# Pooling the keys on TensorE, and another start, in an attention and MLP kernel

## The chip, the cores and the metric

The kernel runs on one core of one Trainium2 chip. The metric is the device time of one execution in microseconds (us). The core has five engines that run their own instruction streams in order and wait for each other by semaphores: TensorE (PE, matrix multiply; PEld is its loading of weights), VectorE (DVE), ScalarE (ACT), GpSimd (POOL) and SyncE (SP). POOL and SP also issue the memory transfers (DMA) of this kernel; the rows POOLq and SPq are these issues. 128 is the number of partitions of the two on-chip memories, SBUF and PSUM; TensorE writes PSUM only.

## The reference

```python
def _attn_ref(q, kv, w_sr):              # q (4, 12288, 128), kv (4, 384, 32, 128)
    r = 4
    kv_pool = kv.reshape(B, H // r, r, W // r, r, C).mean(axis=(2, 4))
    kv_flat = kv_pool.reshape(B, -1, C) @ w_sr         # 768 keys of 128 per batch
    k = v = kv_flat
    s = (q @ k.transpose(0, 2, 1)) / np.sqrt(C)
    a = np.exp(s - s.max(-1, keepdims=True))
    a /= a.sum(-1, keepdims=True) + 1e-09
    return a @ v

def _moe_ref(x, w_in, w_out):            # x (49152, 128), d_ff 2048
    h = x @ w_in
    g = h * (1.0 / (1.0 + np.exp(-1.702 * h)))
    return g @ w_out
```

Each of four batches has 12288 queries and an image of 384 x 32 positions; 4 x 4 positions are averaged to one key, so a batch has 96 x 8 = 768 keys, which serve as values too. All 49152 attention outputs go through one MLP with 2048 hidden channels.

## The kernel before

Queries are worked on in 96 groups of 512. Four groups are a supergroup (2048 queries, 24 of them), and 24 groups are a batch. The 768 keys of a batch are six columns of 128, taken three at a time, so a group is two units (t = 0 and 1) and attention has 192 units. The MLP has 512 units of the same size.

A unit is filled and later drained. `fill_attn` (L171) lets TensorE write three 128 x 512 blocks of scores into a PSUM tile of the pool `big` (two tiles), and ACT takes the exponential of all three into an SBUF tile `ag` (14 tiles). `drain_attn` (L183) multiplies these with the values, six matmuls adding up in a PSUM tile of the pool `ring` (two tiles), and DVE multiplies the sum with the reciprocal row sums and writes it to `xs` (L193). `sums` (L196) is called once per supergroup: 24 matmuls with a narrow matrix of ones (32 columns, one of four column tiles of TensorE for each group) give the row sums in a ring tile, DVE transposes and inverts them (L206 to L210), and POOL spreads them over the partitions (L213) into `rb` (three tiles).

The main loop (L293) fixes the order by hand: step n fills unit n + 2 and drains unit n - 10; after every eighth step come the sums. `manual_schedule` keeps each engine's instructions in the order in which the code is written. `background` (L216), called before each even unit, adds what prepares the next data:

- Queries: `cast_q` (L75) copies a supergroup of q from f32 to bf16 in DRAM, issued on POOL two supergroups ahead. `load_qT` (L80) reads it back transposed into `qT` (two tiles), issued on SP one supergroup ahead.
- Keys of the next batch: `load_kv` (L64) loads an eighth of the image (96 partitions x 2048 f32) on SP into one of three tiles `kvt`. `pool_kv` (L101) adds the 4 x 4 positions with four DVE instructions (L106 to L109). When all eight are done, `transpose_pooled`, `make_k` and `make_v` (L114, L122, L134) transpose on TensorE, multiply with `w_sr` and copy the results to `kT` and `v`; keys and values pass through tiles of `big`.

The start is different for batch 0. POOL issues the cast of the first 512 queries and the first three key loads (cast to bf16 on the way), and then makes the identity matrix `ident`. TensorE pools and transposes at once by multiplying each of the 16 positions of a tile with `ident` and adding up in PSUM (L146 to L157). All 768 keys are made before the first scores. Then come the casts of the other queries of the first supergroup and of the next, and the two weight matrices of the MLP (L160 to L166).

The MLP (`fill_moe`, `drain_moe`, `store`, L243 to L276) starts when the last attention unit is filled, and the change does not touch it.

## Time and profile before

| | us |
|---|---|
| median of three runs | 1095.76 (1087.45 to 1108.19) |
| profiled execution | 1080.91 |
| its span, first to last instruction | 1079.1 |
| queue of hardware transfers (SP), share of 16 engines' span | 23.3% |
| queue of software transfers (POOL), the same | 9.7% |
| mean granted TensorE clock | 0.983 |

Times from the trace, and all sums with them, refer to the profiled execution, whose span is 16.7 us below the median of the three runs. A page of the profile gives busy times by engine, the span in slices, the chain of work that ended last, and groups of instructions by source line with their count, busy time, mean duration in ns and the idle time of the engine before them with its releaser. The other views used below are the timeline (start, duration, instruction, and in brackets the idle time before it and what ended it), the waits (total, how often, longest), and windows (busy time of each engine in a stretch, granted clock, DMA share, GB/s written).

### The profile page before, as it was taken

What the parts mean: (1) busy time and instruction counts of PE and PEld (TensorE: products, weight loads), DVE (VectorE), ACT (ScalarE), POOL (GpSimd) and SP (SyncE); (2) the same over time, 40 slices, a digit from 0 to 9 for tenths busy, and PEclk for the clock granted to TensorE, in tenths of its full rate; (3) what the DMA queues carried; (4) which work ended last, traced back from release to release, by engine and by line L of the source; (5) the groups of instructions that cost most, each with busy time, mean ns of one, the idle gap of its engine ahead of it and who ended that gap; (6) DMA issues with size and microseconds to landing.
All of it is one profiled execution on the core that took longest, in us unless ns stands there. A gap on an engine that the chain in (4) does not pass through costs nothing.

```text
span 1079.1 us, 13408 instructions
## 1 busy us (share of the span) xinstructions
PE 1004.4 (93%) x5368; PEld 461.7 (43%) x5368; DVE 319.0 (30%) x471; ACT 955.2 (89%) x707; POOL 111.6 (10%) x137
## 2 busy tenths in 40 slices
PE   2379978988999999999999999999999999999998
PEld 2224433433444444444444444444444444444443
DVE  0058477347633322222211221122112211221112
ACT  0178877767889999999999999999999999999997
POOL 2124234214323210000000000000000000000000
PEclk9889999989999999999999999999999999999999
DMA  7999399499544001110011101110111101110111
GB/s 109 152 198 186 68 198 184 59 202 167 100 72 85 20 10 40 39 39 36 34 39 39 40 30 39 40 40 31 38 40 39 37 33 39 39 40 30 39 40 39
DMA packets 79790, 74.33 MB, mean 69 GB/s; under 512 B 54496, under 2 KB 57696, under 8 KB 79328
## 3 DMA queue, kind: packets, MB, share of 16 engines
q1 hardware_dynamic: 73520, 56.70, 23.3%
q0 software_dynamic: 6208, 16.78, 9.7%
q8 instruction: 42, 0.69, 0.3%
q14 instruction: 20, 0.16, 0.1%
HBM read 52.49 MB, written 37.75 MB: 84 GB/s over the span
## 4 chain that ended last, share of the span: by engine, by line
PE 83%; DMA 11%; ACT 3%; issue 2%; DVE 1%; SPq 0%; POOL 0%; ACTq 0%; POOLq 0%; DVEq 0%
PE big L247 30%; PE ring L261 30%; PE big L177 9%; PE ring L189 9%; DMA qT<-q_bf 7%; DMA kvt<-in_kv_dram 3%; PE ring L201 2%; ACT ag L180 2%; PE ring L273 2%; ACT ag L250 1%; DMA q_bf<-in_q_dram 1%; DVE kvt L106 0%; SPq L83 0%; ACTq L334 0%; POOL kvt L67 0%
## 5 line engine op out<-in xcount | busy, mean ns | idle before, releaser
L250 ACT ACTIVATE ag<-big 128x1536 bf16<-128x1536 f32 x512 | 689.3, 1555 | 4.7 <-PE big L247 4.6
L247 PE MATMUL big<-x,w_in_sb 128*128 128x512 bf16 x1536 | 414.7, 379 | 0.0
L261 PE MATMUL ring<-ag,w_out_sb 128*128 128x512 bf16 x1536 | 414.2, 379 | 0.5 <-ACT ag L250 0.5
L180 ACT ACTIVATE ag<-big 128x1536 bf16<-128x1536 f32 x192 | 262.9, 1467 | 78.4 <-PE big L177 77.9
L261 PEld LDWEIGHTS <-w_out_sb 128*128 128x128 bf16 x1536 | 150.0, 98 | 181.9 <-issue 0.7
L247 PEld LDWEIGHTS <-w_in_sb 128*128 128x128 bf16 x1536 | 145.8, 98 | 162.4 <-issue 5.0
L265 DVE CAST oT<-ring 128x512 bf16<-128x512 f32 x96 | 66.4, 692 | 450.0 <-PE ring L261 450.0
L177 PE MATMUL big<-qT,kT 128*128 128x512 bf16 x576 | 161.9, 392 | 38.2 <-DMA qT<-q_bf 28.1
L189 PE MATMUL ring<-ag,v 128*128 128x512 bf16 x576 | 159.4, 388 | 7.8 <-DVE x L193 7.6
L213 POOL PARTITION_BROADCAST rb<-t x96 | 93.5, 1025 | 254.1 <-DVE t L210 201.1
L177 PEld LDWEIGHTS <-kT 128*128 128x128 bf16 x576 | 55.1, 100 | 117.6 <-issue 31.9
L193 DVE TENSOR_TENSOR x<-ring,rb 128x512 bf16<-128x512 f32 x96 | 65.2, 688 | 112.4 <-PE ring L189 111.1
L275 DVE CAST o_sb<-ring 128x512 f32<-128x512 bf16 x96 | 66.4, 692 | 101.6 <-PE ring L273 101.6
L189 PEld LDWEIGHTS <-v 128*128 128x128 bf16 x576 | 57.3, 99 | 79.9 <-issue 15.5
L273 PEld LDWEIGHTS <-oT 128*128 128x128 bf16 x384 | 32.2, 114 | 22.7 <-DVE oT L265 1.9
L106 DVE TENSOR_TENSOR kvt<-kvt 96x1024 f32<-96x1024 f32 x24 | 30.5, 1271 | 37.6 <-DMA kvt<-in_kv_dram 37.6
L273 PE MATMUL ring<-ident,oT 128*128 128x128 bf16 x384 | 37.2, 219 | 0.9 <-DVE oT L265 0.8
L201 PE MATMUL ring<-ag,ones 128*32 128x512 bf16 x576 | 35.5, 381 | 0.0
L152 PE MATMUL big<-ident,kvt 96*128 96x96 bf16 x128 | 11.3, 280 | 23.0 <-POOL ident masks.py:199 15.2
L130 ACT CAST kT<-big 128x384 bf16<-128x384 f32 x1 | 0.5, 479 | 34.0 <-DVE kT L129 34.0
L107 DVE TENSOR_TENSOR kvt<-kvt 96x512 f32<-96x512 f32 x24 | 23.4, 976 | 0.8
L201 PEld LDWEIGHTS <-ones 128*32 128x32 bf16 x576 | 13.2, 96 | 21.1 <-issue 10.6
(31 smaller groups left out, 115.7 us busy)
## 6 DMA issues: line engine op xcount, KB each, us to landing
out_dram<-o_sb SPq DMA_DIRECT2D x96, 256.0 KB, 2.0
kvt<-in_kv_dram SPq DMA_DIRECT2D x24, 768.0 KB, 8.6
q_bf<-in_q_dram POOLq DMA_DIRECT2D x23, 512.0 KB, 6.7
kvt<-in_kv_dram POOLq DMA_DIRECT2D x8, 384.0 KB, 6.4
w_in_sb<-in_moe_w_in_dram POOLq DMA_DIRECT2D x1, 512.0 KB, 11.4
w_out_sb<-in_moe_w_out_dram POOLq DMA_DIRECT2D x1, 512.0 KB, 25.4
qT<-q_bf SPq DMA_TRANSPOSE x25, 8.7
q_bf<-in_q_dram POOLq DMA_DIRECT2D x1, 384.0 KB, 7.2
```

The costliest lines, as they stand in the source:

```text
L177: nc.tensor.matmul(s_ps[:, k, :], kTs[b][:, jc * 128:(jc + 1) * 128], rhs, start=True, stop=True)
L180: nc.scalar.activation(a, s_ps, AF.Exp, scale=scale)
L189: nc.tensor.matmul(av_of[i], vs[b][:, jc, :], a_of[i, t][:, k, :], start=(jc == 0), stop=(jc == JC - 1))
L193: nc.vector.tensor_tensor(xs[s][:, (i % 4) * G:(i % 4 + 1) * G], av_of.pop(i), rb_of.pop(i), MUL)
L201: nc.tensor.matmul(ss[32 * gi:32 * gi + 32, :], ones, a_of[4 * s + gi, jc // K][:, jc % K, :], start=(jc == 0), stop=(jc == JC - 1))
L213: nc.gpsimd.partition_broadcast(rb, t2[32 * gi:32 * gi + 1, :])
L247: nc.tensor.matmul(h_ps[:, k, :], w_in_sb[:, fc * 128:(fc + 1) * 128], xs[g // 4][:, (g % 4) * G:(g % 4 + 1) * G], start=True, stop=True)
L250: nc.scalar.activation(a, h_ps, AF.Gelu_apprx_sigmoid)
L261: nc.tensor.matmul(o_of[g], w_out_sb[:, fc, :], a[:, k, :], start=(fc == 0), stop=(fc == FCH - 1))
L265: nc.vector.tensor_copy(oT.rearrange("p a b -> p (a b)"), o_of[g])
L273: nc.tensor.transpose(o_ps[:, gi * 128:(gi + 1) * 128], oT[:, :, gi], ident)
L275: nc.vector.tensor_copy(o_sb.rearrange("p a b -> p (a b)"), o_ps)
```

## The change

The edit has these parts:

1. Pooling moves from DVE to TensorE. A tile of keys is now 128 partitions (rows of the image) x 16 columns of it x 128 channels, in bf16. A matrix `mean4` (128 x 32, 1/16 where partition p belongs to pooled row p // 4) is the weight; four matmuls of 512 columns, one for each of four neighbouring image columns, add up to 32 pooled rows. Three tiles (`ch`) fill three column tiles of TensorE, 96 pooled rows, half of a batch's keys (`a`).
2. Keys and values are made by halves, with ring tiles of PSUM instead of big ones. For batches 1 to 3 the steps stand at fixed groups of the batch before (9, 10, 12, 13 for the first half, 17, 18, 20, 21 for the second), after the drain.
3. All key loads are issued on POOL, with a cast to bf16: six of 1 MB (f32) per batch, at groups 2, 4, 6, 11, 13, 15. For batch 0 they go to `xs` tiles that are written much later.
4. Batch 0 starts with the first half of its keys. The order of the first eight units is changed: t = 0 of groups 0 to 3, then t = 1 of them, and the second half of the keys is made before the fifth unit.
5. The queries of the first two supergroups (4096) are loaded straight to SBUF with a cast and transposed on TensorE; ACT copies the first four groups from PSUM, DVE the next four. For the others `load_qT` is issued two supergroups ahead (three `qT` tiles) and `cast_q` three ahead.
6. `ident` and `mean4` are made on POOL before any load. The MLP weights are loaded at groups 40 and 64. `ag` has 15 tiles.

```diff
-    kv_r = kv.rearrange("b (hp r1) (wp w1) c -> b wp hp r1 (w1 c)", r1=r, w1=r)
+    kv_r = kv.rearrange("b (ch p) (a w) c -> b a ch p (w c)", p=128, a=2)
...
-    qpool = ctx.enter_context(tc.tile_pool(name="qpool", bufs=2))
-    agpool = ctx.enter_context(tc.tile_pool(name="ag", bufs=14))
+    qpool = ctx.enter_context(tc.tile_pool(name="qpool", bufs=3))
+    agpool = ctx.enter_context(tc.tile_pool(name="ag", bufs=15))
...
+    def load_kv(b, a, ch):
+
+        t = xs[NS - 1 - a * HC - ch] if b == 0 else kvload.tile([128, SG], BF, name="kvt")
+        nc.gpsimd.dma_start(out=t, in_=kv_r[b, a, ch])
+        kv_tiles[b, a, ch] = t.rearrange("p (wp w1 c) -> p w1 wp c", w1=r, c=C)
+
+    def pool_kv(b, a):
+
+        ps = ring.tile([128, 512], F32, name="ring")
+        ts = [kv_tiles.pop((b, a, ch)) for ch in range(HC)]
+        order = ([(ch, w) for ch in range(HC) for w in range(r)] if b == 0 else
+                 [(ch, w) for w in range(r) for ch in range(HC)])
+        for ch, w in order:
+            nc.tensor.matmul(ps[32 * ch:32 * ch + 32, :], mean4, ts[ch][:, w],
+                             start=(w == 0), stop=(w == r - 1))
+        pooled[b, a] = kvtmp.tile([Hp, 4, C], BF, name="pooled")
+        nc.vector.tensor_copy(pooled[b, a].rearrange("p a c -> p (a c)"), ps[:Hp, :])
...
+    def transpose_q(g):
+        s = g // 4
+        if g % 4 == 0:
             qTs[s] = qpool.tile([128, 1, SG], BF, name="qT")
...
+        ps = ring.tile([128, 4, 128], BF, name="ring")
+        for i in range(4):
+            o = (g % 4) * G + i * 128
+            nc.tensor.transpose(ps[:, i, :], xs[NS // 2 + s][:, o:o + 128], ident)
+        dst = qTs[s][:, 0, (g % 4) * G:(g % 4 + 1) * G].rearrange("p (t i) -> p i t", i=4)
+        if s == 0:
+            nc.scalar.copy(dst, ps)
+        else:
+            nc.vector.tensor_copy(dst, ps)
...
+    load_q(0, 0, 1)
+    for ch in range(HC):
+        load_kv(0, 0, ch)
+    load_q(0, 1, 4)
+    for ch in range(HC):
+        load_kv(0, 1, ch)
+    load_q(1, 0, 4)
+    cast_q(2)
+    cast_q(3)
...
+    transpose_q(0)
+    pool_kv(0, 0)
+    transpose_pooled(0, 0)
+    make_k(0, 0)
+    load_qT(2)
...
-            if s + 1 < NS:
-                load_qT(s + 1)
-            if s + 2 < NS:
-                cast_q(s + 2)
...
+            if 3 <= s + 2 < NS:
+                load_qT(s + 2)
+            if 4 <= s + 3 < NS:
+                cast_q(s + 3)
+        if b + 1 < B and gb in (2, 4, 6, 11, 13, 15):
+            a, ch = divmod((2, 4, 6, 11, 13, 15).index(gb), HC)
+            load_kv(b + 1, a, ch)
...
+    units = [(i, t) for t in range(2) for i in range(4)] + [(i, t) for i in range(4, NG) for t in range(2)]
+
     def fill(n):
         if n < NA:
+            i, t = units[n]
             if n % 2 == 0:
                 background(n // 2)
-            fill_attn(n // 2, n % 2)
+            if n < 8:
+                if t == 0 and i > 0:
+                    transpose_q(i)
+                if n == 4:
+                    make_v(0, 0)
+                    pool_kv(0, 1)
+                    transpose_pooled(0, 1)
+                    make_k(0, 1)
+                if n == 6:
+                    make_v(0, 1)
+                if n == 7:
+                    transpose_q(4)
+                    transpose_q(5)
+            fill_attn(i, t)
...
+        elif n < NA and n % 2 == 1:
+            if n in (9, 11):
+                transpose_q(6 + (n - 9) // 2)
+            extra(n // 2)
```

The order of the instructions on three queues shows what moved. The rows give the line, the operation, what it writes and reads, its shape and the semaphores that it waits for (DMASW and DMAHW are those of transfers issued by software on POOL and by hardware on SP). On POOL, at the program's start, before:

```order
L77 DMA q_bf<-in_q_dram 16x4096
L67 DMA kvt<-in_kv_dram 96x4x512 x3
masks.py:197 MEMSET ident 128x128
masks.py:199 ISA
masks.py:199 AFFINE_SELECT ident<-ident 128x128 [waits Pool_49]
```

and on POOL at the same place now (mean_118 is `mean4`; x_99 and x_105 to x_110 are tiles of `xs` that hold queries and keys for a while):

```order
masks.py:197 MEMSET ident 128x128
masks.py:199 ISA
masks.py:199 AFFINE_SELECT ident<-ident 128x128 [waits Pool_49]
L145 MEMSET mean_118 128x32
L146 AFFINE_SELECT mean_118<-mean_118 128x32 [waits Pool_49]
L148 AFFINE_SELECT mean_118<-mean_118 128x32 [waits Pool_49]
L122 DMA x_99<-in_q_dram 128x512
L69 DMA x_110<-in_kv_dram 128x2048
L69 DMA x_109<-in_kv_dram 128x2048
L69 DMA x_108<-in_kv_dram 128x2048
```

The identity matrix stood behind the first four loads; now it and `mean4` stand ahead of every load. On SP, the first transposed queries and key loads before:

```order
L83 DMA_TRANSPOSE qT<-q_bf 128x1x2048 [waits DMASW2_49]
L70 DMA kvt<-in_kv_dram 96x4x512 [waits DMASW6_49,DMASW3_49,PE_49]
L70 DMA kvt<-in_kv_dram 96x4x512 [waits DMASW7_49,DMASW4_49,PE_49]
L70 DMA kvt<-in_kv_dram 96x4x512 [waits DMASW5_49,DMASW0_49,PE_49]
L70 DMA kvt<-in_kv_dram 96x4x512 [waits DMAHW4_49,DVE_49]
L83 DMA_TRANSPOSE qT<-q_bf 128x1x2048 [waits DMAHW1_49,DMAHW0_49,DMAHW2_49,DMASW5_49,PE_49]
```

and on SP now:

```order
L141 DMA w_sr_f<-in_w_sr_dram 128x128
L118 DMA_TRANSPOSE qT<-q_bf 128x1x2048 [waits DMASW1_49]
L118 DMA_TRANSPOSE qT<-q_bf 128x1x2048 [waits DMASW2_49,PE_49,Activation_49]
L118 DMA_TRANSPOSE qT<-q_bf 128x1x2048 [waits DMASW4_49,DVE_49,PE_49]
L118 DMA_TRANSPOSE qT<-q_bf 128x1x2048 [waits DMAHW1_49,DMASW7_49,PE_49]
```

The key loads that waited for DVE are gone from between the transposes. On DVE, between two supergroups while the keys of batch 1 are made, before:

```order
L106 TENSOR_TENSOR kvt<-kvt 96x1024 [waits DMASW5_49,DMAHW6_49,DMASW2_49,DMASW0_49]
L107 TENSOR_TENSOR kvt<-kvt 96x512 [waits DVE_49]
L108 TENSOR_TENSOR kvt<-kvt 96x256 [waits DVE_49]
L109 TENSOR_TENSOR pooled<-kvt 96x128 [waits DVE_49]
L193 TENSOR_TENSOR x_87<-ring,rb 128x512 [waits PE_49,Pool_49]
```

and on DVE now:

```order
L197 TENSOR_TENSOR x_88<-ring,rb 128x512 [waits PE_49,Pool_49]
L82 CAST pooled<-ring 96x512 [waits PE_49]
L197 TENSOR_TENSOR x_88<-ring,rb 128x512 [waits PE_49,Pool_49]
L90 COPY pT<-ring 128x384 [waits PE_49]
L197 TENSOR_TENSOR x_88<-ring,rb 128x512 [waits PE_49,Pool_49]
```

The additions that wait for a transfer ahead of a normalising multiply are gone; single copies that wait for TensorE take their place, and the wait for the key transfers is on TensorE's pooling matmuls (L79).

More of the change, by code (lines that the diff above doesn't have):

```diff
@@ new lines, in transpose_pooled, with make_k @@
+    def transpose_pooled(b, a):
+        ps = ring.tile([128, 4, Hp], BF, name="ring")
+        t = pooled.pop((b, a))
+        for wp in range(4):
+            nc.tensor.transpose(ps[:, wp, :], t[:, wp, :], ident[:Hp, :Hp])
+        pTs[b, a] = kvtmp.tile([128, h], BF, name="pT")
+        nc.vector.tensor_copy(pTs[b, a], ps.rearrange("p a b -> p (a b)"))
+    def make_k(b, a):
+        ps = ring.tile([128, 512], F32, name="ring")
+        if a == 0:
+            kTs[b] = kvres.tile([128, J], BF, name="kT")
+        nc.tensor.matmul(ps[:, :h], w_sr_sb, pTs[b, a], start=True, stop=True)
+        nc.vector.tensor_copy(kTs[b][:, a * h:(a + 1) * h], ps[:, :h])
@@ L73, with make_v, cast_q @@
+    def make_v(b, a):
+        ps = ring.tile([128, 512], F32, name="ring")
+        if a == 0:
+            vs[b] = kvres.tile([128, JC, C], BF, name="v")
+        pT = pTs.pop((b, a))
+        for k in range(K):
+            nc.tensor.matmul(ps[:, k * C:(k + 1) * C], pT[:, k * 128:(k + 1) * 128], w_sr_sb,
+                             start=True, stop=True)
+        nc.vector.tensor_copy(vs[b][:, a * K:(a + 1) * K, :].rearrange("p k c -> p (k c)"), ps[:, :h])
     qTs = {}
-    def cast_q(s, lo=0, n=SG):
-        sl = slice(s * SG + lo, s * SG + lo + n)
+    def cast_q(s):
+        sl = slice(s * SG, (s + 1) * SG)
@@ L134, in make_v @@
-    def make_v(b):
-        pT = pTs.pop(b)
-        v_ps = big.tile([128, K, 512], F32, name="big")
-        vs[b] = kvres.tile([128, JC, C], BF, name="v")
-        for jc in range(JC):
-            nc.tensor.matmul(v_ps[:, jc // 3, (jc % 3) * C:(jc % 3 + 1) * C],
-                             pT[:, jc * 128:(jc + 1) * 128], w_sr_sb, start=True, stop=True)
-        nc.vector.tensor_copy(vs[b].rearrange("p (a b) c -> p a (b c)", a=2), v_ps[:, 0:2, :h])
-    p_ps = big.tile([128, K, 512], F32, name="big")
```

111 lines of the change are left out of this document (30 added, 81 removed).

## The prediction

> **What bounds the kernel now.** I read the page first: busy shares, the granted clock by slice, the chain that ended last.
>
> ```profile
> span 1079.1 us, 13408 instructions
> PE 1004.4 (93%) x5368; PEld 461.7 (43%) x5368; DVE 319.0 (30%) x471; ACT 955.2 (89%) x707; POOL 111.6 (10%) x137
> ...
> PEclk9889999989999999999999999999999999999999
> ...
> PE 83%; DMA 11%; ACT 3%; issue 2%; DVE 1%; SPq 0%; POOL 0%; ACTq 0%; POOLq 0%; DVEq 0%
> ```
>
> TensorE is busy 93% of the span, and 11% of the chain is DMA. Where that 11% lies is read from the windows view (columns: stretch, its length, busy us of each engine with counts, granted clock, DMA share, GB/s).
>
> ```profile
> 186.60:193.20 6.60, 4.69 (x12) 1.64 (x12) 0.00 (x0) 2.03 (x2) 0.00 (x0) 0.50 0.65 119
> 64.33:379.22 314.89, 286.92 (x1699) 121.97 (x1699) 177.41 (x264) 252.55 (x186) 98.01 (x112) 0.97 0.72 128
> 379.22:1079.10 699.88, 694.48 (x3505) 325.47 (x3504) 138.68 (x201) 689.15 (x512) 2.91 (x4) 1.00 0.10 37
> ```
>
> The last 699.88 us (the MLP) have ACT busy for 689.15 and TensorE for 694.48: nothing to gain there, and the edit leaves them alone. 64.33 and 379.22 are where the first and the last of the 24 row-sum blocks start; the timeline gives the first, the chain of waits (start, duration, what) two late neighbours.
>
> ```profile
> 64.33 1.48 PE L201 MATMUL ring<-ag,ones 128*32 128x512 bf16 x24
> ```
>
> ```profile
> 355.43 1.41 PE ring L201 x24
> ...
> 367.36 1.41 PE ring L201 x24
> ```
>
> Undisturbed, one block follows another after 367.36 - 355.43 = 11.93 us. The 23 intervals should take 23 x 11.93 = 274.4, and they take 314.9: **40.5 us too many**. TensorE's waits in that stretch (view of waits: us in total, times, longest):
>
> ```profile
> PE big L177 <- DMA qT<-q_bf: 14.0, 4, 4.5
> PE ring L189 <- DVE x L193: 7.6, 2, 4.1
> PE big L177 <- ACT ag L180: 6.1, 7, 1.0
> PE ring L189 <- DVE t L206: 0.2, 1, 0.2
> ```
>
> That is 27.9. The other 12.6 are the key and value matmuls and matmuls at half clock after a wait: the 186.60 window shows a granted 0.50, so about half of its 4.69 busy us is lost. Without sums a group of eight units is 48 matmuls in 11.93 - 1.41 = 10.52, 0.219 each; keys and values are 2304 columns a batch, 4.5 such matmuls, about 1.0, and with their weight loads I say 1.1, or 3.4 for three batches. What lies ahead, 0 to 64.33, is the third pot: start-up.
>
> **What goes: the two kinds of waits.** The transposed queries are late because SP issues them one supergroup ahead, behind key loads that wait for buffers. Now SP issues nothing else during attention, two supergroups ahead, with a third buffer; casts run three ahead. The wait on the normalising multiply comes from DVE standing behind a key tile:
>
> ```profile
> 228.59 1.22 DVE L106 TENSOR_TENSOR kvt<-kvt 96x1024 f32<-96x1024 f32 x1 [4.84 <-DMA kvt<-in_kv_dram]
> ...
> 231.22 1.28 DVE L193 TENSOR_TENSOR x<-ring,rb 128x512 bf16<-128x512 f32 x2
> ...
> 231.96 1.44 PE L189 MATMUL ring<-ag,v 128*128 128x512 bf16 x3 [4.07 <-DVE x L193]
> ```
>
> DVE held L193 back for a late key tile and TensorE then waited 4.07. The four DVE additions per key tile are gone. Of the 6.1 on ACT, about 3.6 are the bubbles of key and value results in the pool that ACT drains; they move to the other PSUM pool. I keep 2.5, the filling of the pipeline.
>
> **What is added to TensorE.** Pooling now costs, for batches 1 to 3, six blocks of 12 matmuls, three abreast: four rounds. The 24 row-sum matmuls run four abreast, six rounds in 1.41, so a block is 4/6 x 1.41 = 0.94, and six are 5.6. If they ran singly a block would be 12 x 0.219 = 2.6; hidden it cannot be, as TensorE is the bound here; the row with the same tiling is nearest, so 0.94. Four query transposes per group go by the MLP's:
>
> ```profile
> L273 PE MATMUL ring<-ident,oT 128*128 128x128 bf16 x384 | 37.2, 219 | 0.9 <-DVE oT L265 0.8
> L201 PE MATMUL ring<-ag,ones 128*32 128x512 bf16 x576 | 35.5, 381 | 0.0
> L201 PEld LDWEIGHTS <-ones 128*32 128x32 bf16 x576 | 13.2, 96 | 21.1 <-issue 10.6
> ```
>
> 37.2 / 96 = 0.39 per group; two groups fall in this stretch, 0.8. Narrow weight loads take 96 ns and lie beside matmuls. The Trainium skill (TensorEngine Tiling (Array Packing), Key Properties and Restrictions) says that a change of tiling mode drains the array and that column tiling turns fast weight load off; if that laid the 12 loads of 96 ns of a block open, 1.15 x 6 = 6.9 us would come on top, 1064. The trace speaks against it: 24 loads of the same narrow form fit inside 1.41.
>
> **POOL's queue.** It gets 18 key loads of about 0.67 us issue time; DVE and TensorE wait for its partition broadcasts, which now stand behind loads that wait for a key buffer. A buffer is freed by pooling matmuls that stand two groups of queries ahead of the load, about 3 us (2 x 11.93 / 8), so I price this at nothing; that margin is its cover, and if it goes, broadcasts and then the multiply are late next. The stretch becomes 274.4 + 3.4 (keys, values) + 2.5 + 5.6 + 0.8 + 2.0 for waits that I can't name = **288.7**, against 314.9: 26.2 less. The 2.0 lies between 0 and a late tile at each of six blocks (rival 4).
>
> **Start-up.** It decides the rest, and here POOL's order matters. Timeline, POOL:
>
> ```profile
> 1.22 0.63 POOL L77 DMA_DIRECT2D q_bf<-in_q_dram  x1 [0.79 <-POOLq L323]
> 1.85 2.04 POOL L67 DMA_DIRECT2D kvt<-in_kv_dram  x3
> 3.88 0.22 POOL masks.py:197 MEMSET ident<- 128x128 bf16 x1
> ...
> 14.82 0.28 POOL masks.py:199 TENSOR_SCALAR_AFFINE_SELECT ident<-ident 128x128 bf16<-128x128 bf16 x1 [10.71 <-issue]
> ```
>
> The mask operation stands still for 10.71 us with nothing shown that it waits for. Before, four loads were already issued; now all loads stand behind it. The Trainium skill (GPSIMD Engine Reference, Instruction dispatch) has the first call of a freshly loaded kernel pay a code load of about 6 us that shows no instruction; by it the sum would be 4.7 lower.
>
> Loads then start at 1.22 + 0.22 + 10.71 + 0.28 + about 0.8 (three small mask operations, each at most 0.28) = 13.2. Rates by the windows view, and times from issue to landing (last column of the page's list of transfers):
>
> ```profile
> 20.00:25.00 5.00, 1.46 (x16) 1.25 (x16) 0.56 (x1) 0.00 (x0) 0.79 (x2) 1.00 1.19 191
> 304.00:306.00 2.00, 2.00 (x11) 0.89 (x10) 0.69 (x1) 2.00 (x3) 0.40 (x2) 1.00 1.49 262
> ```
>
> ```profile
> qT<-q_bf SPq DMA_TRANSPOSE x25, 8.7
> ...
> q_bf<-in_q_dram POOLq DMA_DIRECT2D x1, 128.0 KB, 3.1
> ```
>
> The first queries (128 KB) land 3.1 later, at 16.3. Three key tiles of 0.52 MB at 191 GB/s take 8.2: 24.5 (at 262 GB/s, 22.3). I take 191, the rate of key loads. The chain from there goes by these rows:
>
> ```profile
> 34.10 0.52 PE L127 MATMUL big<-pT,w_sr_sb 128*128 128x384 bf16 x1
> 34.34 0.56 DVE L157 CAST pT<-big 128x384 bf16<-128x384 f32 x1 [10.49 <-PE big L152]
> ...
> 36.06 0.48 ACT L130 CAST kT<-big 128x384 bf16<-128x384 f32 x1 [34.05 <-DVE kT L129]
> ...
> 37.12 2.72 PE L177 MATMUL big<-qT,kT 128*128 128x512 bf16 x6 [1.05 <-DVE v L141]
> ...
> 38.59 2.79 ACT L180 ACTIVATE ag<-big 128x1536 bf16<-128x1536 f32 x2 [2.06 <-PE big L177]
> 53.88 2.74 PE L177 MATMUL big<-qT,kT 128*128 128x512 bf16 x6 [14.04 <-DMA qT<-q_bf]
> ```
>
> TensorE is slow here (0.45 us a matmul against 0.22 later). The last tile's four pooling matmuls 1.8, cast 0.7 (0.56 x 512/384), transposes 0.4, copy 0.56, key matmul 0.5, cast 0.56, first scores 1.36: 30.4. Three more units, each exp 1.40, query copy on ACT 0.6 (0.48 x 512/384) and scores 1.36 in a row, since one engine does both copy and exp: 40.5 cold, 38.4 with scores at 0.66; 39.5. Then the second half of keys, landed by 24.5 + 1.96 MB / 191 GB/s = 34.8: values, 12 pooling matmuls (2.6 to 5.4), casts, keys, scores, together 8.2: 47.7. Four exps of 1.345 (689.15 / 512) and the tenth unit's scores: **first sums at 53.7**, say 53, against 64.33, where 14.04 were a wait for queries.
>
> **Sum.** 53.0 + 288.7 + 699.9 = 1041.6, against 1079.1: 37.5 less. The profiled execution itself took 1080.91 and the three runs shown 1087 to 1108, median 1095.76; I carry the difference over, 1095.76 - 37.5 = 1058, and say 1057.
>
> **Rivals.**
> 1. *The pause at the mask is shorter*, because four loads ran beside it before and none does now. Between 0 and 10.71 the middle is 5.4 less: 1052. Against it: the only row says 10.71. By the 6 us of the Trainium skill (GPSIMD Engine Reference, Instruction dispatch) it would be 1053.
> 2. *The start is slower than summed*: each step at its cold price (1.0 more up to the fourth scores, 1.4 more in the second pooling block) and loads that share 191 GB/s with the query loads and casts behind them (4 to 5 more): first sums at 60, 1064.
> 3. *The queries are still late*: the change doesn't do what it says. If casts and key loads on the other queue slow the transposes, 14.0 of waits and the half clock, 12.6 - 3.4 = 9.2, stay: 1080, within 2%. For it: the longest took 23.1 to land, as long as two supergroups (23.9). Against: the median is 8.7, and key tiles are half the bytes on chip.
> 4. *Slower*: TensorE itself, in order, now waits for key tiles where DVE did. A tile is issued six to seven units (9 us) ahead of its block. A late one costs its lateness and 2.3 of half clock. The six must cost 6.3 each to eat the gain, so from a landing of 13 us on it is no gain; at the longest landing seen, 16.4, they cost 6 x (7.4 + 2.3) = 58: 1115. Against: the medians below.
>
> ```profile
> kvt<-in_kv_dram SPq DMA_DIRECT2D x24, 768.0 KB, 8.6
> ...
> kvt<-in_kv_dram POOLq DMA_DIRECT2D x8, 384.0 KB, 6.4
> ```
>
> The transposed queries' own view, then the key tiles':
>
> ```profile
> DMA to landing us min/median/max: 4.1/8.7/23.1
> ```
>
> ```profile
> DMA to landing us min/median/max: 4.7/8.1/16.4
> ```
>
> **How the numbers follow.** The forecast as summed has 0.44 (1048 to 1066), rival 1 0.25, rival 2 0.15, rival 3 0.12, rival 4 0.04. Low end: rival 1 with loads at 262 GB/s (2.2), full clock (2.5) and no unnamed waits (2.0) is 1045, and the runs shown lie up to 12 from their median: 1034. High end: rival 2 and those 12 is 1076; 1077, just short of rival 3. Faster by over 2% (about what a measurement of this kernel can tell from no change) is under 1074: forecast, rivals 1 and 2 make 0.84. Rival 3 and half of rival 4 lie within 2%, 0.14; slower 0.02.
>
> **What would show it.** Right: first row sums near 53, the last 289 later; no wait of score matmuls on queries nor of value matmuls on the multiply; pooling blocks of 0.94; the pause at the mask operation ahead of the first load. Wrong: pooling matmuls that wait for key tiles after the start, half clock in the middle of attention, or an MLP that is not 700 us long.

## The result, and the profile after

The changed kernel takes 1042.83 us (median of four runs, 1041.73 to 1043.32). Four runs of the kernel before have a median of 1094.79 (1087.45 to 1108.19). The ratio is 0.9545, 95% interval 0.9497 to 0.9593; ratios, here and below, leave out runs over 1.5% above the fastest of their kernel, which the medians keep. The profiled execution took 1043.32, with a span of 1041.6.

The page of the changed kernel: span, busy time by engine, granted clock by slice, engines of the chain that ended last, and one row of its groups.

```profile
span 1041.6 us, 13332 instructions
PE 1005.0 (96%) x5376; PEld 457.3 (44%) x5376; DVE 260.3 (25%) x398; ACT 962.7 (92%) x710; POOL 99.7 (10%) x156
...
PEclk9599999999999999999999999999999999999999
...
PE 95%; ACT 2%; issue 1%; DVE 1%; DMA 1%; POOL 0%; ACTq 0%; POOLq 0%; DVEq 0%
...
L136 ACT COPY qT<-ring 128x512 bf16<-128x512 bf16 x4 | 5.1, 1286 | 11.4 <-PE ring L133 11.4
```

TensorE is as busy as before (1005.0 against 1004.4 us), though it has taken on the pooling: by the pages' rows the value matmuls, some of which ran at half clock after a wait before, take 379 ns in the mean and took 388. DVE has lost 59 us of work. The chain's share of DMA fell from 11% to 1%, and the only slice with a low clock is the second, in the start.

The windows view, cut as in the prediction: first row sums to last, then the rest.

```profile
52.00:341.06 289.06, 285.40 (x1779) 122.45 (x1779) 114.66 (x185) 254.37 (x186) 87.43 (x129) 1.00 0.61 105
341.06:1041.60 700.54, 695.47 (x3505) 325.54 (x3504) 138.54 (x201) 689.92 (x512) 2.92 (x4) 1.00 0.10 37
```

Before, the first stretch took 314.89 with 286.92 us of TensorE work. Now it takes 289.06 with 285.40: 28.0 us without work have become 3.7. What is left of TensorE's waits there is one line:

```profile
PE big L181 <- DVE qT L138: 3.3, 2, 1.8
```

No score matmul waits for a transfer any more, and no value matmul for the multiply. The 3.3 are the queries of the second supergroup, which DVE copies from PSUM. Undisturbed, the blocks of row sums follow each other as before, as two rows of the chain of waits show (11.93 apart):

```profile
118.41 1.41 PE ring L205 x24
130.34 1.41 PE ring L205 x24
```

Groups of instructions by line, for TensorE in the stretch from 52.00 to 341.06 (busy us in all, mean ns of one, idle time before them):

```profile
L79 PE MATMUL ring<-kvt,mean 128*32 128x512 bf16 x72 | 6.3, 382 | 0.0
L88 PE MATMUL ring<-ident,pooled 96*128 96x96 bf16 x24 | 2.0, 205 | 0.0
L105 PE MATMUL ring<-w_sr_sb,pT 128*128 128x128 bf16 x18 | 2.0, 219 | 0.0
L96 PE MATMUL ring<-pT,w_sr_sb 128*128 128x384 bf16 x6 | 2.0, 326 | 0.0
...
L133 PE MATMUL ring<-ident,x 128*128 128x128 bf16 x8 | 0.8, 219 | 0.0
```

Six pooling blocks cost 6.3 us, none waited, and keys and values cost 6.0.

The start, from the timeline (start, duration, instruction, idle time before it and what ended it):

```profile
8.83 0.28 POOL masks.py:199 TENSOR_SCALAR_AFFINE_SELECT ident<-ident 128x128 bf16<-128x128 bf16 x1 [7.84 <-issue]
9.70 0.86 POOL L122 DMA_DIRECT2D x<-in_q_dram  x1
20.85 1.50 PE L79 MATMUL ring<-x,mean 128*32 128x512 bf16 x4 [0.64 <-DMA x<-in_kv_dram]
24.90 1.15 PE L181 MATMUL big<-qT,kT 128*128 128x512 bf16 x3 [0.65 <-DVE kT L97]
26.08 1.45 ACT L184 ACTIVATE ag<-big 128x1536 bf16<-128x1536 f32 x1 [11.27 <-PE big L181]
27.43 1.28 ACT L136 COPY qT<-ring 128x512 bf16<-128x512 bf16 x1
28.76 1.44 PE L181 MATMUL big<-qT,kT 128*128 128x512 bf16 x3 [2.29 <-ACT qT L136]
38.76 1.92 PE L79 MATMUL ring<-x,mean 128*32 128x512 bf16 x12
43.58 2.74 PE L181 MATMUL big<-qT,kT 128*128 128x512 bf16 x6 [0.65 <-DVE kT L97]
52.00 1.48 PE L205 MATMUL ring<-ag,ones 128*32 128x512 bf16 x24
```

The mask operation paused for 7.84 and not 10.71. The exponential, the query copy of 1.28 and the scores then stand in a row for each of the first units: 28.76 - 24.90 is nearly 4. The first sums start at 52.00, against 64.33 before.

So by the spans the gain is 12.3 in the start and 25.8 in the stretch of attention, with 0.7 lost in the MLP.

### The profile page after: what moved, and what is told of

The parts are those of the page before. It is cut to its first block, busy times and chain, and to the rows that moved or that the text cites. A ratio compares the mean times of both kernels' runs of the same rounds, so it can differ in the third digit from the quotient of the medians.

```text
span 1041.6 us, 13332 instructions
## 1 busy us (share of the span) xinstructions
PE 1005.0 (96%) x5376; PEld 457.3 (44%) x5376; DVE 260.3 (25%) x398; ACT 962.7 (92%) x710; POOL 99.7 (10%) x156
## 4 chain that ended last, share of the span: by engine, by line
PE 95%; ACT 2%; issue 1%; DVE 1%; DMA 1%; POOL 0%; ACTq 0%; POOLq 0%; DVEq 0%
PE big L256 32%; PE ring L270 31%; PE big L181 13%; PE ring L193 12%; PE ring L205 3%; PE ring L282 2%; ACT ag L259 1%; PE ring L79 1%; DMA x<-in_kv_dram 1%; ACT ag L184 1%; ACT qT L136 0%; DVE qT L138 0%; PE ring L88 0%; PE ring L96 0%; PE ring L105 0%
## 5 line engine op out<-in xcount | busy, mean ns | idle before, releaser
L181 PE MATMUL big<-qT,kT 128*128 128x512 bf16 x576 | 160.0, 388 | 12.2 <-ACT qT L136 6.9
L193 PE MATMUL ring<-ag,v 128*128 128x512 bf16 x576 | 154.8, 379 | 0.4
L217 POOL PARTITION_BROADCAST rb<-t x96 | 72.8, 797 | 231.8 <-DVE t L214 184.3
L210 DVE STREAM_TRANSPOSE t<-ring 128x512 f32<-128x512 f32 x24 | 17.2, 717 | 17.8 <-PE ring L205 17.8
L214 DVE STREAM_TRANSPOSE t<-t 128x512 f32<-128x512 f32 x24 | 17.1, 711 | 3.2 <-DVE t L212 0.9
L133 PE MATMUL ring<-ident,x 128*128 128x128 bf16 x32 | 4.3, 288 | 12.9 <-DMA x<-in_q_dram 12.9
L136 ACT COPY qT<-ring 128x512 bf16<-128x512 bf16 x4 | 5.1, 1286 | 11.4 <-PE ring L133 11.4
```

Of the source, the lines that this page charges most:

```text
L181: nc.tensor.matmul(s_ps[:, k, :], kTs[b][:, jc * 128:(jc + 1) * 128], rhs, start=True, stop=True)
L193: nc.tensor.matmul(av_of[i], vs[b][:, jc, :], a_of[i, t][:, k, :], start=(jc == 0), stop=(jc == JC - 1))
L217: nc.gpsimd.partition_broadcast(rb, t2[32 * gi:32 * gi + 1, :])
```

## The experiments

Two questions: which part of the change took the waits out of attention (theory: moving transfers between the queues; rival: pooling on TensorE), and what the start still hangs on. The kernels that came out, each beside runs of the kernel before on the same chip; "first sums" and "to the last sums" are from the profiled execution:

| kernel | median us (runs) | ratio to before, 95% | first sums | to the last sums |
|---|---|---|---|---|
| before | | | 64.3 | 314.9 |
| queries ahead | 1079.02 (10) | 0.997, 0.993 to 1.002 | 66.1 | 311.3 |
| keys on POOL | 1069.29 (5) | 0.991, 0.988 to 0.995 | 65.6 | 300.6 |
| both, pooling on DVE | 1067.52 (4) | 0.987, 0.981 to 0.993 | 66.7 | 296.4 |
| changed kernel, pooling on DVE | 1045.02 (4) | 0.966, 0.960 to 0.971 | 51.2 | 291.5 |
| changed kernel, again | 1042.20 (4) | 0.964, 0.959 to 0.968 | 50.1 | 289.1 |
| tile by tile | 1042.35 (4) | 0.963, 0.958 to 0.969 | 50.9 | 289.2 |
| one ahead | 1042.05 (4) | 0.963, 0.957 to 0.969 | 50.3 | 289.0 |
| keys in one piece | 1046.26 (4) | 0.966, 0.959 to 0.974 | 55.2 | 289.6 |
| contiguous copies on DVE | 1035.95 (4) | 0.959, 0.955 to 0.963 | 46.2 | 287.5 |
| loads before the masks | 1038.96 (4) | 0.962, 0.959 to 0.965 | 47.8 | 289.0 |
| both of these | 1029.96 (4) | 0.952, 0.948 to 0.956 | 41.4 | 287.5 |
| masks through DRAM | 1040.46 (4) | 0.961, 0.955 to 0.966 | 44.0 | not read |

### Queries ahead, and nothing else

The kernel before, with the transposed queries two supergroups ahead (`ag` gives up a tile to make room for the third `qT`):

```diff
-    qpool = ctx.enter_context(tc.tile_pool(name="qpool", bufs=2))
-    agpool = ctx.enter_context(tc.tile_pool(name="ag", bufs=14))
+    qpool = ctx.enter_context(tc.tile_pool(name="qpool", bufs=3))
+    agpool = ctx.enter_context(tc.tile_pool(name="ag", bufs=13))
...
-                load_qT(s + 1)
+                load_qT(s + 2)
...
-                cast_q(s + 2)
+                cast_q(s + 3)
```

> The kernel before, with the transposed queries issued two supergroups ahead (three tiles, 13 exponential tiles instead of 14 to make room) and their casts three ahead; keys as before. My theory: the late queries and the DVE wait are two separate losses. Of the 14.0 us of waits on queries after the first sums most go, with some 5 of the half clock behind them; the 7.6 on the multiply stay, and so does the start: span about 18 below the kernel before. Rival: the SP queue is held up by key loads that wait for DVE, so an earlier place in it does not help: 0 to 4 below.

Measured: 1079.02 against 1083.63, no difference that can be told: the rival's 0 to 4 less, but not for its reason. TensorE's waits after its first sums:

```profile
PE ring L191 <- DVE x L195: 17.6, 5, 5.3
PE big L179 <- ACT ag L182: 6.0, 7, 1.0
PE ring L191 <- DVE t L208: 2.0, 1, 2.0
```

The 14.0 us of waits on queries are gone, and the wait on the multiply has grown from 7.6 to 17.6. In the code SP's key loads now stand behind transposes that are issued earlier (the first key load of batch 1 is issued at 63.17, where it was at 56.82), and DVE, which adds up key tiles ahead of the multiply, waits for them. DVE's waits on key tiles in attention, before:

```profile
DVE kvt L106 <- DMA kvt<-in_kv_dram: 37.6, 4, 28.1
```

and with the queries ahead:

```profile
DVE kvt L106 <- DMA kvt<-in_kv_dram: 51.1, 6, 32.7
```

The longest of each is the idle time before the first tile; the rest grew from 9.5 to 18.4. The gain turned into the other wait. Neither theory had said this: the two waits of the prediction are not two independent pots, since transposes and key loads delay each other in one queue. (The missing `ag` tile, here and in the kernel with both moves, was not tried alone.)

### Keys on POOL, and nothing else

```diff
-            t = kvload.tile([Hp, r, r * C], F32, name="kvt")
-            nc.sync.dma_start(out=t, in_=kv_r[b, wp])
+            t = kvload.tile([Hp, r, r * C], BF, name="kvt")
+            nc.gpsimd.dma_start(out=t, in_=kv_r[b, wp])
```

> The kernel before, with the key tiles of batches 1 to 3 cast to bf16 and loaded on POOL; queries still one supergroup ahead on SP, pooling still on DVE. My theory: SP is free of waits, so most of the 14.0 us on queries go, and smaller tiles come sooner, so part of the 7.6 on the multiply goes: span about 1060. Rival: one supergroup ahead is too short whatever stands on SP: 1075.

Measured: 1069.29 against 1079.18, 9.9 less: under 2%, with an interval that excludes no change, and between the theory's 1060 and the rival's 1075. TensorE's waits in the same stretch:

```profile
PE big L177 <- ACT ag L180: 8.0, 9, 1.0
PE big L177 <- DMA qT<-q_bf: 6.1, 2, 3.2
PE ring L189 <- DVE x L193: 4.1, 2, 2.2
```

The edit shortens both waits: queries from 14.0 to 6.1, the multiply from 7.6 to 4.1. For the queries that is the other half of the same finding, since SP now issues transposes alone. For the multiply it is not settled: DVE still waits 12.2 for key tiles after its first one (9.5 before), but the tiles are bf16 now, and the four additions of a tile take 1.95 us by their medians where they took 2.96. The queue and the type were not tried apart.

### Both, with the pooling still on DVE

The two edits above in one kernel.

> The kernel before, with the keys of batches 1 to 3 on POOL in bf16 and the queries two supergroups ahead (13 exponential tiles): both moves of the tried pair at once, pooling still on DVE and the start as it was. If the two waits hang together through SP's queue, the pair removes what neither does alone: no wait on queries after the first sums and under 5 us on the multiply, 1060 to 1065 and runs within 3 us of each other. If DVE's pooling alone keeps the waits, they stay at 10 us or more: 1069 as with the keys alone.

Measured: 1067.52 against 1083.42, 15.9 less, again under 2%; from first sums to last 296.4 against 314.9. The theory's 1060 to 1065 was missed, and its runs within 3 us of each other too: they spread by 12.6.

```profile
PE big L179 <- ACT ag L182: 7.9, 9, 1.0
PE ring L191 <- DVE x L195: 5.7, 2, 3.0
PE ring L203 <- DVE x L195: 2.4, 2, 2.0
```

No wait on queries is left. So 18.5 of the 25.8 us that the change gains in attention come with the two moves (bf16 tiles included), on the old pooling; that is by one profiled execution of each kernel. What is left are waits on ACT (by the code, keys and values pass through the PSUM pool that ACT drains) and on DVE, which still waits 18.7 for late key tiles.

### The changed kernel, with the pooling of batches 1 to 3 on DVE

```diff
+        nc.vector.tensor_tensor(t[:, 0:2, :], t[:, 0:2, :], t[:, 2:4, :], ADD)
+        nc.vector.tensor_tensor(t[:, 0, :], t[:, 0, :], t[:, 1, :], ADD)
+        nc.vector.tensor_tensor(t[:, 0, 0:2 * C], t[:, 0, 0:2 * C], t[:, 0, 2 * C:4 * C], ADD)
+        nc.vector.tensor_tensor(pooled[b, a][:, x, :], t[:, 0, 0:C], t[:, 0, C:2 * C], ADD)
...
+        if b + 1 < B and gb % 2 == 0 and gb < 16:
+            load_old(b + 1, gb // 2)
+        if b + 1 < B and gb % 2 == 1 and 5 <= gb < 21:
+            pool_old(b + 1, (gb - 5) // 2)
...
-    for a, gbs in enumerate(((9, 10, 12, 13), (17, 18, 20, 21))):
-        for gb, f in zip(gbs, (pool_kv, transpose_pooled, make_k, make_v)):
+    for a, gbs in enumerate(((12, 13, 14), (20, 21, 22))):
+        for gb, f in zip(gbs, (transpose_pooled, make_k, make_v)):
```

The old tiles, in bf16, are loaded on POOL and added up five groups later; keys and values keep the new PSUM pool.

> The changed kernel, with batches 1 to 3 pooled on DVE again (bf16 tiles of the old shape, loaded on POOL with a cast, four tiles, each issued five groups ahead of its additions); start, queries and halves as changed, the factor 1/16 moved to w_sr. If pooling on DVE is what hurts, waits on the multiply come back, 4 to 8 us: 1040 to 1045, less the pooling matmuls. If it was only the late key tiles, they stay away and TensorE saves its six blocks of 0.98: 1035.

Measured: 1045.02. On the same chip the next two kernels, whose pooling is on TensorE, took 1042.35 and 1042.05. So pooling on TensorE, the part that names the change, is worth about 2.8 us. TensorE's waits from first sums to last show where DVE's additions still cost something, and the timeline the longest of them:

```profile
PE big L198 <- DVE qT L155: 5.9, 2, 4.1
PE ring L210 <- DVE x L214: 4.4, 3, 1.7
```

```profile
57.00 1.27 DVE L155 COPY qT<-ring 128x512 bf16<-128x512 bf16 x1
...
58.33 1.46 PE L198 MATMUL big<-qT,kT 128*128 128x512 bf16 x3 [4.08 <-DVE qT L155]
```

The wait on the multiply is back with 4.4. The query copy of the second supergroup stood behind additions, and TensorE waited 4.08 for it. The profiled span of the kernel with both moves is 1064.4, and this one's is 1043.2. Of these 21.2, the changed start makes 15.5 (first sums at 51.2 and 66.7) and attention 4.9, where the ring's PSUM tiles for keys and values, the additions' later place, a fourth key tile and two more `ag` tiles come in together; they were not tried apart.

### Pooling matmuls tile by tile, and queries one ahead

Two small edits of the changed kernel. The first takes the order for batches 1 to 3 that only batch 0 had, in which four matmuls of one column tile follow each other:

```diff
-        order = ([(ch, w) for ch in range(HC) for w in range(r)] if b == 0 else
-                 [(ch, w) for w in range(r) for ch in range(HC)])
+        order = [(ch, w) for ch in range(HC) for w in range(r)]
```

> The changed kernel, with the pooling matmuls of batches 1 to 3 in the order of batch 0: four on one column tile, then four on the next. If TensorE starts matmuls strictly in order, each waits for its own column tile and a block takes 12 x 0.22 = 2.6 us instead of 0.98: six blocks, 10 us more, span 1051. If column tiles work their own queues (the second block of batch 0 took 1.90 at half clock in this order, where 12 x 0.427 would be 5.1), a block stays at 1.0 and the span at 1041.

Measured: 1042.35, no difference from the changed kernel. A block of twelve, in the timeline:

```profile
72.23 1.06 PE L78 MATMUL ring<-kvt,mean 128*32 128x512 bf16 x12
```

In the alternating order a block took 1.04. The three column tiles overlap whichever way the matmuls are issued: one after the other, twelve would take 12 x 0.219 = 2.6.

The second takes the longer lead of the queries away:

```diff
-            if 3 <= s + 2 < NS:
-                load_qT(s + 2)
+            if 3 <= s + 1 < NS:
+                load_qT(s + 1)
```

> The changed kernel, with load_qT issued one supergroup ahead instead of two; everything else stays, so SP still issues nothing else. If the free SP queue is what makes the queries come in time, waits on them stay under 3 us in all (a transpose lands in 8.5 us in the median, 15.6 at most, and has 12): span 1041 to 1045. If the second supergroup of lead is needed, waits of 3 to 4 us come back at most supergroups, with half clock behind them: 1055 or more.

Measured: 1042.05, and no wait on a transposed query tile in the trace (the second supergroup's copies on DVE still cost 3.8). With SP free of key loads one supergroup of lead is enough; the third `qT` tile buys nothing here.

### Batch 0's keys in one piece

All keys of batch 0 ahead of the first scores, and units in plain order:

```diff
     make_k(0, 0)
+    make_v(0, 0)
+    pool_kv(0, 1)
+    transpose_pooled(0, 1)
+    make_k(0, 1)
+    make_v(0, 1)
     load_qT(2)
...
-    units = [(i, t) for t in range(2) for i in range(4)] + [(i, t) for i in range(4, NG) for t in range(2)]
+    units = [(i, t) for i in range(NG) for t in range(2)]
```

> The changed kernel, with all 768 keys of batch 0 made before the first scores and the units in their plain order; loads, query transposes and everything later as changed. It takes back the halves alone. If the halves are worth what the later first scores cost, those start some 6 us later (near 30.6) and so does all that follows: span 1047. If the copies on ACT and the break before the second half (ACT idle from 40.0 to 45.1) eat most of it, the first sums move by 1 to 2 us only: 1043.

Measured: 1046.26, 4.1 above the changed kernel.

```profile
34.24 2.77 PE L186 MATMUL big<-qT,kT 128*128 128x512 bf16 x6
```

The first scores start 9.3 later than in the changed kernel (24.90), but the first sums only 3.2 to 5.1 later (55.2 against 52.0 and 50.1). They had been expected at 30.6; the second half's pooling follows its tiles as they land, the last at 30.06. The halves give back half of their head start, since the first four units then run at the pace of exponential, copy and scores in a row. So the halves are 3 to 5 of the 12.3 that the start gains; the rest, in which the 14.04 wait for transposed queries went, was not tried apart.

### The query copies: contiguous and on DVE

In the changed kernel a copy from PSUM writes elements 8 bytes apart, since a load puts four neighbouring queries on one partition. Here the load puts query i x 128 + p on partition p, so the transposes come out in order:

```diff
-rearrange("(g p i) c -> p g (i c)", p=128, i=4))
+rearrange("(g i p) c -> p g i c", p=128, i=4))
...
-        dst = qTs[s][:, 0, (g % 4) * G:(g % 4 + 1) * G].rearrange("p (t i) -> p i t", i=4)
-        if s == 0:
-            nc.scalar.copy(dst, ps)
-        else:
-            nc.vector.tensor_copy(dst, ps)
+        dst = qTs[s][:, 0, (g % 4) * G:(g % 4 + 1) * G]
+        nc.vector.tensor_copy(dst, ps.rearrange("p i t -> p (i t)"))
```

> The changed kernel, with the first four groups' query copies on DVE and contiguous (queries loaded in an order that makes the transposes land in place; the output is the reference's). My theory: at the start ACT does a 1.28 us copy and a 1.45 us exp in series with the scores, 4.16 us per unit; with the copy beside the exp a unit takes about 2.1 to 2.9, so 4 to 6 us less, first sums near 47, span 1036 to 1038; the copy itself falls from 1.28 to about 0.7 if the 8-byte steps are what makes it slow. Rival: the second half of the keys lands late (after 36), and TensorE waits for it instead: no more than 1 us less.

Measured: 1035.95, 6 to 7 below the changed kernel (1042.20 and 1042.83 in its two sets). Timeline of the start:

```profile
27.89 0.42 DVE L135 COPY qT<-ring 128x512 bf16<-128x512 bf16 x1 [1.98 <-PE ring L133]
28.37 1.44 PE L178 MATMUL big<-qT,kT 128*128 128x512 bf16 x3 [0.52 <-DVE qT L135]
...
30.76 1.46 PE L178 MATMUL big<-qT,kT 128*128 128x512 bf16 x3 [0.52 <-DVE qT L135]
```

The copy takes 0.42 and no longer 1.28, and a unit follows the other after 2.39 us (30.76 - 28.37) and no longer about 4.2. The second supergroup's copies, on DVE in both kernels, took 1.26 to 1.33 with the 8-byte steps, so on DVE the step makes the copy three times as long. On ACT no contiguous copy of this shape was run; the nearest row is 0.48 for 384 columns (L130 of the kernel before).

### Loads before the masks, and both of these

The changed kernel, with the first query load and the first three key loads issued ahead of `ident` and `mean4`:

```diff
+    load_q(0, 0, 1)
+    for ch in range(HC):
+        load_kv(0, 0, ch)
     ident = cpool.tile([128, 128], BF)
     make_identity(nc, ident)
```

> The changed kernel, with the first query load and the first three key loads issued on POOL ahead of the identity and the mean matrix. If transfers beside it stretch the pause at the mask, it is near 10.7 again, the matrices are ready at about 15.5 and the first scores start near 20 instead of 24.9: span about 1037. If the pause is 7.8 whatever runs beside it, they are ready near 13 and the first scores start near 17.5: span about 1034. If the loads are what the pause waits for, it grows with their number and nothing is won: 1041.

Measured: 1038.96, 3 to 4 below the changed kernel.

```profile
14.89 0.28 POOL masks.py:199 TENSOR_SCALAR_AFFINE_SELECT ident<-ident 128x128 bf16<-128x128 bf16 x1 [11.06 <-issue]
```

The pause is 11.06 with four loads issued ahead of it, where it was 7.84 with all of them behind it, and 10.71 in the kernel before, which also had four ahead. Over all profiled executions with the mask on POOL it is 10.71 to 11.70 in the six with loads ahead and 7.13 to 7.84 in the seven without. The loads now run during the pause, and the first scores start earlier, at 20.69 where they started at 24.90:

```profile
20.69 1.46 PE L181 MATMUL big<-qT,kT 128*128 128x512 bf16 x3 [0.65 <-DVE kT L97]
```

Both edits in one kernel:

> The changed kernel with both edits of the start: query copies on DVE and contiguous, and the first four loads ahead of the masks. If the two savings lie one after the other on the chain, they add up: first scores near 20.7, four units at 2.4 us, second pooling block near 28.5, first sums near 40, span 1029. If the second half of the keys, issued after the masks, lands after 30, TensorE waits for it and 3 to 4 us are lost again: 1033.

Measured: 1029.96, 12.2 below the changed kernel beside it and the fastest of all. The timeline's rows for it:

```profile
15.37 0.28 POOL masks.py:199 TENSOR_SCALAR_AFFINE_SELECT ident<-ident 128x128 bf16<-128x128 bf16 x1 [11.32 <-issue]
...
16.35 1.92 PE L79 MATMUL ring<-x,mean 128*32 128x512 bf16 x12
...
29.98 1.06 PE L79 MATMUL ring<-x,mean 128*32 128x512 bf16 x12
...
41.40 1.48 PE L202 MATMUL ring<-ag,ones 128*32 128x512 bf16 x24
```

All three key tiles have landed when the masks are ready; the first pooling block follows the mask at once. What holds the start now is the pause of the mask operation.

### The masks through DRAM

To take that pause away, `ident` and `mean4` are written to DRAM as zeros and a diagonal, and read back, all on SP (in the kernel with the contiguous copies); POOL starts with loads.

```diff
-    make_identity(nc, ident)
+    nc.sync.dma_start(out=id_d.rearrange("(p x) -> p x", x=129), in_=zeros[:, 0:129])
+    nc.sync.dma_start(out=id_d.rearrange("(p x) -> p x", x=129)[:, 0:1], in_=dg[:, 0:1])
+    nc.sync.dma_start(out=ident, in_=id_d[0:128 * 128].rearrange("(p x) -> p x", x=128))
```

(`mean4` goes the same way.)

> As the kernel with query copies on DVE, and the two mask matrices made without POOL: DVE writes zeros and a column of constants, and SP writes and reads them through a small DRAM buffer whose row is one element longer than the matrix row, so that the constants land on the diagonal. POOL has no mask operation and starts with the loads. Theory: the pause of 7.8 to 11.1 us belongs to the first mask operation and falls away, loads start at 1.3, the matrices are there after three transfers in a row (about 2 us each, 8 us), first scores near 18, first sums near 37: span 1025. Rival: the pause belongs to POOL's first instructions and shows up ahead of the first load or in the DRAM round trip, which shares the queues with 2.5 MB of loads and then takes 12 us or more: 1030 or above.

Measured: 1040.46 (1036.92 to 1054.38), no gain over the 1035.95 of the kernel that it starts from; the middle of the other three runs is 1037.52. The profiled execution, at 1054.38, is the highest of the four, so only its start and one late tile are read from it.

```profile
1.25 0.92 POOL L122 DMA_DIRECT2D x<-in_q_dram  x1 [0.81 <-POOLq L357]
...
18.08 0.59 PE L133 MATMUL ring<-ident,x 128*128 128x128 bf16 x4 [18.08 <-DMA ident<-id_d]
...
158.19 1.87 PE L79 MATMUL ring<-kvt,mean 128*32 128x512 bf16 x10 [18.34 <-DMA kvt<-in_kv_dram]
```

The pause is gone with the operation, and the identity arrives at 18.08, later than the pause would have ended: the DRAM round trip of the rival. The list of transfers says why:

```profile
ident<-id_d SPq DMA_DIRECT2D x1, 32.0 KB, 7.4
...
id_d<-dg SPq DMA_DIRECT2D x1, 0.2 KB, 7.6
```

Two small transfers, one after the other, took 7.6 and 7.4 from issue to landing, where a write of 32.2 KB issued ahead of the loads took 1.7. The first of the two is written in pieces of 2 bytes; whether that or the loads beside it make it slow was not tried. The last timeline row is the prediction's rival 4 in one execution of another kernel: a key tile came late, TensorE stood still for 18.34, and its granted clock was 0.62 in the 6 us afterwards. Its key loads are those of the changed kernel, so such a wait can come there too, though none of its two profiled executions has it.

### The changed kernel again

> The changed kernel once more, on the chip of the other three. Its runs lay within 1.6 us of each other (1041.7 to 1043.3) where those of the kernel before lay within 21. If the scatter of the kernel before comes from its waits on transfers, this one is within 2 us of 1042 here too; if it was the chip of that day, it scatters.

Measured: 1042.20 against 1083.42, ratio 0.964 (0.959 to 0.968): 41.2 us, where the first comparison had 52.0. The changed kernel repeats to within 1 us; the kernel before does not.

## Why the prediction was right, and which terms were mis-sized

**The sum on the profiled execution held.** Predicted 53.0 + 288.7 + 699.9 = 1041.6; measured 52.00 + 289.06 + 700.54 = 1041.6. That the total agrees to a tenth is partly luck: the start was summed to 53.7 and rounded down to 53.0 (with 53.7 the total is 1042.3), and errors cancel inside it, as the points below show. The measured 1042.83 lies in the range, but below the 1048 to 1066 that the forecast as summed was given. Two slips of arithmetic do not bear on this: 1057 - 4.7 is 1052, where rival 1 has 1053, and 1045 - 12 is 1033, where the low end is 1034.

**The steady stretch.** The step "the two kinds of waits go" is right, and both causes were named rightly: no wait on a transposed query tile, none on the multiply, full clock. The additions on top of 274.4 were 14.3 by prediction, and the stretch shows 289.06 - 274.4 = 14.7. Within them: pooling 6.3 (5.6 predicted), keys and values 6.0 (3.4), query transposes 0.8 (0.8), waits on ACT none (2.5), waits nobody had named 3.3 (2.0; they are the slow query copies). By their rows these add up to 16.4, so some 2 us of them lie beside each other. The keys were priced by their columns; these small matmuls come singly, and by the rows they are about twice as long (a 384-column one 326 ns, where columns alone give 0.219 x 384/512 = 164). What the prediction did not see is that the two waits are tied by one queue: the first experiment removed one and got the other. Since the change moves both, the sum did not suffer.

**Pooling at 0.94 a block.** Right: a block took 1.04. The six blocks took 6.3 in all with no idle time before them, so nothing of the size of the 6.9 shows that the prediction named as the price of weight loads laid open. The Trainium skill (TensorEngine Tiling (Array Packing), Key Properties and Restrictions) says that a change of tiling mode drains the array and that column tiling turns fast weight load off. The trace shows no price for either. The Trainium skill's statement in the same section, Key Properties, that tiles operate independently agrees with the twelve matmuls that took 1.04 and 1.06 in two orders.

**POOL's queue at nothing.** Right: no wait on a broadcast and none on a key tile in the profiled execution after 52 us. The margin of 3 us was misread, though: fills run two units ahead of the step that pools, so the load that takes over a buffer stands one step behind the pooling block and not two groups. In the trace it starts 0.6 after that block ends (74.92 against 73.32 + 1.04). What covered it is the distance to the next broadcasts, which start at 83.40.

**The start.** Predicted 53.7, measured 52.00, by errors that cancel. First scores ended at 26.0 and not 30.4: 2.9 of these 4.4 are the pause at the mask, taken at 10.71 and measured at 7.84 (rival 1, in part). An earlier first instruction and quicker small masks make 0.6, a quicker chain behind the last key tile 0.7. The next three units took 12.5 and not 9.1: the query copy was taken at 0.6, from a contiguous copy, and was 1.28, which makes 2.0 of the 3.4, and the rest is mostly the scores, which stayed at 1.44 a unit where half had been taken at 0.66. The second pooling block was put at 2.6 to 5.4 and took 1.92, so that stage took 6.4 and not 8.2. The last stage, up to the first sums, took 1.0 more. In all: -4.4 + 3.4 - 1.8 + 1.0, about 1.7 less than the 53.7. The Trainium skill (GPSIMD Engine Reference, Instruction dispatch) has about 6 us for the first call of a freshly loaded kernel. The traces show 7.13 to 7.84 with the loads behind it and 10.71 to 11.70 with four ahead; no run shows whether this pause is that call's.

**The median: the term that was mis-sized.** The prediction carried over the 16.7 us by which the median shown stood above the profiled span. That offset was not the chip's, and the new kernel does not have it: its median is 1.2 above its span. The 1095.76 itself was high: 34 later runs of the kernel before, in four sets, have medians of 1079.18 to 1083.63, and the profiled 1080.91 lies among them. Without the carry-over the prediction would have been 1041.6 and about 2 for what lies around the span. So 1057 was 14.2 too high, and this term is all of it: 1057 - 1041.6 = 15.4 were put between span and median, and 1.2 are there. On one chip the two kernels lie 41.2 apart, where the sum by spans had 37.5.

**Why the kernel before scatters is argued, not shown.** Its 38 runs go from 1071 to 1108, 36 of them to 1096. The kernels with waits on late transfers in mid-attention spread too (queries ahead by 13.5 us, keys on POOL by 6.6, both by 12.6, masks through DRAM by 17.5), and those without such waits by 0.9 to 2.1. The kernel with contiguous copies is an exception (4.9, no such wait in its profile), and it is unexplained. Also open is why the two edits of the start together gain some 2 us more than apart; that is less than the 4.9 by which the runs of the kernel with contiguous copies spread, and about the 1.9 between the first sums of the changed kernel's two profiled executions, so it may be no effect of the edits.

## What to carry to other kernels

When waits on two different things in one stretch both go back to transfers of one queue, look at them together: here an earlier place in the queue for one moved the lateness to the other (1079.02, no gain), and taking one off the queue shortened both (1069.29). Sum a prediction on the profiled execution, and carry an offset between it and a few scattered runs over only if the scatter would survive the change. In a start-up chain every copy on an engine that is in series with the rest counts fully, so look at the access steps of the small copies before the big transfers.

## What the hardware showed that was not expected

- Column tiles overlap whatever the order in which their matmuls are issued: twelve took 1.04 alternating and 1.06 tile by tile in attention, where the granted clock is 1.00, and 1.92 tile by tile in the start of the changed kernel at a granted clock of 0.50.
- The granted clock of a short window does not always tell TensorE's pace: in the kernel with both edits of the start it reads 1.00 for the block of 1.92 (from 16.35) and for the one of 1.06 (from 29.98).
- A copy of 128 x 512 bf16 from PSUM that writes elements 8 bytes apart took 1.28 on ACT and up to 1.33 on DVE; the contiguous one took 0.42 on DVE.
- The pause of the first mask operation on POOL is stretched by loads issued ahead of it: 7.13 to 7.84 without, 10.71 to 11.70 with four.
- A transfer of 0.2 KB in 2-byte pieces took 7.6 from issue to landing beside large loads, and a read of 32 KB took 7.4.
